# First query group: its value spans cut out of the row tiles by TensorE instead of loaded from memory, in another issue sequence

## The chip, the cores and the metric

The kernel runs on one core of a Trainium2 chip. The metric is the device time of one execution in microseconds (us). Shorter is better.

The engines are TensorE (PE in the profile, its weight loads PEld), VectorE (DVE), ScalarE (ACT), GpSimd (POOL) and SyncE (SP), which here issues all DMAs.

## The reference

Attention with a local window and pooled blocks, followed by a feed-forward layer with softplus, all in float32 (the weights of the second part arrive as 64-bit floats).

```python
batch, n_heads, seq, head_dim = 4, 8, 768, 64
block, window = 32, 16
k_sum = k.reshape(B, H, nb, block, D).max(axis=3)
v_sum = v.reshape(B, H, nb, block, D).mean(axis=3)
scores_l = scale * q @ k^T          # kept where abs(i - j) < 16, else -1e9
scores_s = scale * q @ k_sum^T + log(block)
a = softmax(concat(scores_l, scores_s))
attn = a @ concat(v, v_sum)
x = attn as (3072, 512)
out = softplus(x @ w_in) @ w_out    # w_in 512 x 2048, w_out 2048 x 512
```

## The kernel before

**Tiles.** Queries go in chunks of 256 (three to a batch, twelve in all), heads in pairs (`hp`, four pairs, so 128 rows hold two heads). Two chunks make a group `x` (six groups). Inside a chunk each window of 64 queries sees a span of 96 keys and the 24 block sums of its batch, so that a score row has 120 columns. One attention block treats one chunk and two head pairs. For the first group there are four such blocks, in this order: chunk 0 with head pairs 0 and 1 (called **A0** here), chunk 1 with the same pairs (**A1**), then chunks 0 and 1 with head pairs 2 and 3 (**B0**, **B1**).

**One block.** PE writes scores (`sc`, L642), DVE adds the mask and finds the maxima (L655, eight instructions), ACT takes exponentials (L663, eight), DVE inverts the sums (L670, L671), DVE or POOL normalizes (L676; ACT in eight steps at L679). For the first group PE transposes with an identity (`pt`, L696), ACT copies the result to SBUF (`pT`, L700), PE multiplies with the values (`xo`, L740), ACT rounds the result into `xw` (L770) and DVE writes the rest beside it (L774). Later groups transpose in squares by DVE and a round trip through memory (`tb`, `squares`).

**The first group's inputs.** `FirstPlaces` loads per head pair the queries (L556, 256 KiB) and the eight value spans of two chunks (L564): seven that lie 64 rows apart and one at the start, as a DMA of 336 KiB and one of 48 KiB, eight DMAs in all, 1536 KiB, in runs of 512 bytes. The 24 block means of v come from `declare_first_values`: six row tiles `vn0` of 128 x 512 (L424, 256 KiB each, also in runs of 512 bytes, so all of batch 0's v is in SBUF once), six matmuls with a 0/1 matrix that add up each 32 rows (`vt`, L429), one scaled copy (L440, `v0`), and per head pair a copy of that 24 x 128 block beside each of its eight spans (L570, 24 x 1024 elements). Keys come as `kf0` (L404, 384 KiB per head pair).

**Feed-forward.** For a group, `ph` (L1058) is x @ w_in for one of 16 row blocks `f` of the hidden layer, 12 matmuls with three rounding terms; ACT takes the softplus twice (`gh` rounded at L1160, exact at L1164), DVE the difference (`gl`, L1168), and `po` (L1175) is the product with w_out. Weights are loaded in pairs (L918, L911: 512 KiB or 1024 KiB) and unpacked from 64 bits by DVE, ACT and POOL. Half of the weights is loaded at the start, beside the first group's inputs; the first group's `ph` follows block B1 at once.

**Order.** `SEQUENCE` is a list of numbers: it names each step, and with a letter the engine that takes it. It fixes the order on every engine and on SP's queue. Each engine runs its own list in order and waits at the first step whose input is missing. SP's DMAs use eight semaphores in turn, so that a DMA is issued only when the eighth one before it has landed. `warm` (L1249) are 40 matmuls without use, placed in gaps of PE. The banks `po` (four, also used by `pt` and `xo`) and `ph` (two) are PSUM.

Of the kernel before, what the change touches and what calls it, by code (L numbers as in the profile page):

```python
# [152 lines left out]
98 179 97 185 85 83 113 138 99 106 324 211 114 186 204a 325 326a 372 115 350 42 103 116 227 126b 117 187a 369 127 200a
129 212 327 201 217 128 130 386 351 131 120 118 188a 387b 134 132 352 119 328 121 133 139 135 228 373 214 353 246 202
370 146 371a 140 385 247 248 374 249 250 376 203 255 392a 229 256 257 329 395 251 378 205 258 315 317 321 330 259 354b
355 262 320 396 263 143a 316 215 380 332 232 206 207 375a 218 318 331 414b 269 230 149 264 270 252 253 254 265 377
141a 260 271 356 272 397 266 219a 261 333 381 273 382 398 413 343 357 346 420a 267 360 216 220 415a 221 334 276 399b
336 231 359 379 345 423 348 358 223 222 277 344 400 349 507 508b 283 284 233 512a 424 224 268 236 401 278 279 509b 280
285 286 515 361 237 425 287 234a 235 388 383a 426 533 384 147 534a 274 362 402 389 290 535b 538a 238a 405 391 225 403
291 427a 226a 239 428 390 393 394 404 516 297 298 292 275 293 541 294 406 240 299 241 338a 429 142 687 144 242 243 281  # L160
430 407a 282 300 517 560b 301 364a 244a 431 432 518 519b 245 366 433 411a 566a 561b 416 288 422 289 520 412a 542 417
418 543 295 296 302 419 408 421 559 434 150 337 569 409a 521 410a 435a 367 439 365 304 305 437 339a 510 306a 511 522
524 544 588b 309a 310a 440a 438a 545b 303 525 441 442 587 443 594a 546 450 514 523 570 589 444 451 145 452 513 453 597
571 148 445 307a 526 681 547 685 527a 536 454 689 446 572 540 699 548 682 447 686 457 573a 705 551 683 690 458 698 539
550 549 448 529a 537 464 574 598 449 455 459 700a 460 684 465 466 456 462 575 467 693 599 461 552 468 562 708 688a 576
600 471 601 530a 727 691 553a 567 565 472 563 478 473 602 709 694 479 578 463 557a 564 726 531 728a 532a 474 480 481
475 482 555a 710 469 579 733 577 470 363 692a 711 568 736 755 756b 580 485 712a 581 151 603 754 486 476 713 759 604
605 477 590 585 606 595 586 596 558a 492 593 335 583a 487 493 488 737 591 738 489 494 528 739 483 584 592 495 607 762
608 484 740b 490 491 695 556a 714 308 781a 496 498 785 715 696 609 611a 613a 612a 614a 782b 701 718 436 615 616 617
780 741 703 311 763 618 497 499 716 697 500 501a 624 625 504a 930 502 764 619 702 620 742 707 717 631 765 766 788 610  # L170
626 621 767 873b 622 934 632 627 628 638 789 879 872 704 639 874b 633 634 640 635 882 505a 641 706 901a 928 642 719
623 629 768 902 743 790 791 645 646 729 732 931a 731 647 630 648 720 722 745 636 554 734 730 746 637 649 724a 744 735
932 747 900 929 936 748 652 792 653 757 793 883 643 884 769 758 772 770 644 933 885 907a 659 886 654 503 655 752 660
771 656 661 937 650 662 760 794 761 773 774 910 938 940 795 721 935 651 663 798 666 797 945 778 783 657 658 667 946b
786 784 664 796 787 665 887 750 939 799 911 947a 952 912 888 955 913 875 723 668 776a 889 973 941 669 881 506 914b 876
670 779 751a 753a 800a 804a 725 777 974b 890 880 878 802a 671 975a 805 892 803a 877 806 815 675a 807 891 808 915 809
956 916 816 817 980a 810 672 818 673 983 893 917 674 957 919 1068 819 678a 822 582 894a 903 920 679a 1067 676 906 1069
942 811 918 823 958 959a 812 908 909 904 960 984 829 813 985 824 1072a 986 830 825 814 895 775 826 943 820 987 831 832
896 905 821 827 961 921 833 1399 948 944 988 989 1075 922a 1076 1077 1078 1079 962 951 836 837 680 1080 843 844 838
845 954 964 949 1092b 846 839 1096a 898 953 965 1093 840 963 1091 828 834 835 841 677 950 1099 899 847 801 1100 926a  # L180
1116 966 976 990 967a 993 982 842 848 849 969 971a 1117a 979 1122a 897a 972 968 850 851 1101 981 1115 924a 925 852 853
977 857 858 854 991 992 855 859 978 1081 1102 994 860 995 1533 749 1125 1103a 1070 970 856 997a 1400 927a 999 861 1082
996 1085 862 1071 1074 1084 1104 866 1000 998a 864 1142 1001 865 1002 1003 1141 1010 1073 1004 923 869a 1148a 870 1011
1012 863 1083 1013 1105 1126 1143 1005 1014 1151 1086 1127 867a 1094 1006 1087 1007 1128 1089 1090 1097 1095 1401a
1129 1088 1106 1008 1098 1109 1017 1018 1019 1020 1024 1025 1021 1026 1130 1152 1027 1108 871 1009 1031 1032 1033
1534a 1028 1107 1034 1035 1131 1015 1110 1405 868 1402 1153 1154 1111 1113 1539 1016 1118 1114 1132 1124 1022 1023
1112 1038 1039 1535 1133 1045 1040 1135 1409 1041 1155b 1029 1119 1121 1120 1123 1042 1030 1156 1046 1134 1136 1047
1157 1048 1139 1036 1144 1037 1146 1049 1145 1052 1406 1137 1158 1053 1412 1043 1054 1150 1161 1055 1056 1160 1140
1149 1147 1536 1044 1159 1050 1543 1138 1540a 1051 1058 1059 1162 1057 1163 1165 1164 1061 1064 1166 1167 1168 1176
1169 1177 1060 1170 1178 1171 1225 1062 1172 1183 1184 1179 1226a 1180 1190 1243 1185 1065 1191 1244 1173 1245 1174  # L190
1227 1261 1228 1229 1246 1192 1186 1175 1193 1187 1194 1248a 1181 1247 1266 1234 1197 1182 1204 1205 1198 1262 1239a
1410a 1249 1230 1188 1066 1189 1250 1195 1252 1280 1063 1235a 1263 1264 1236 1265 1253a 1237 1238 1240 1231 1199 1267
1200 1206 1232 1196 1270 1251 1201 1207 1233a 1208 1211 1212 1281a 1282 1268 1218 1213 1214 1257a 1283 1202 1271 1203
# [39 lines left out]
def kernel(  # L233
# [301 lines left out]
    class FirstPlaces:  # L535


        def __init__(self, hp, sums, own, sp):
# [4 lines left out]
            def place(g):  # L543
                return own[g]().rearrange("p two n c -> p (two n c)")
# [803 lines left out]
```

## Time and profile before

| | us |
|---|---|
| three runs | 627.8, 628.35, 630.74 |
| median | 628.35 |
| the profiled execution, whole time | 630.65 |
| its span, first to last instruction | 628.9 |
| PE busy | 607.4 (97% of the span) |
| DVE / ACT / POOL busy | 387.8 / 349.3 / 179.9 |

The page gives busy times over the whole span. The first 60 us hold the loading and attention of the first group, and there no engine is busy all the time; from then on PE is.

### The profile page before, as it was taken

To read this page: it belongs to the slowest core of one execution; us is meant where nothing else is said; L and a number is where in the kernel's file an instruction comes from. 1 tells how busy PE (TensorE), PEld (TensorE's weight loads), DVE (VectorE), ACT (ScalarE), POOL (GpSimd) and SP (SyncE) were. 2 spreads that over 40 slices of the span, in tenths; PEclk is the share of its full clock that TensorE was granted. 3 is DMA by queue.
4 is the path that set the end of the run, shared out by engine and by line. 5 is a ranking of instruction groups with operands and counts; after the bars stand their busy time and mean duration, and the time that the engine had idled before them with its cause. 6 is when DMAs were issued, how large, how long until landed. Compare 5 with 4: busy or idle time off the path is not lost.

```text
span 628.9 us, 12000 instructions
## 1 busy us (share of the span) xinstructions
PE 607.4 (97%) x4452; PEld 507.5 (81%) x4452; DVE 387.8 (62%) x1010; ACT 349.3 (56%) x859; POOL 179.9 (29%) x180
## 2 busy tenths in 40 slices
PE   7669999999999999999999999999999999999997
PEld 6357778787887888888888888889889888989895
DVE  5989988676455765444225579874665664464542
ACT  4799999869567677556436887442212322132211
POOL 5334354041323213121000644474410224103000
PEclk9987999999999999999999999999999999999999
DMA  8997877977857776657435640023040240030031
GB/s 292 289 271 211 226 223 229 267 213 222 265 170 249 204 225 219 206 170 233 132 91 190 194 172 3 1 82 111 10 168 2 100 134 1 27 108 1 31 105 67
DMA packets 66570, 96.12 MB, mean 153 GB/s; under 512 B 5872, under 2 KB 44624, under 8 KB 65744
## 3 DMA queue, kind: packets, MB, share of 16 engines
q1 hardware_dynamic: 66512, 95.36, 49.2%
q8 instruction: 35, 0.57, 0.4%
q14 instruction: 23, 0.19, 0.1%
HBM read 66.06 MB, written 27.26 MB: 148 GB/s over the span
## 4 chain that ended last, share of the span: by engine, by line
PE 82%; ACT 7%; SPq 4%; DVE 4%; DMA 3%; issue 1%; ACTq 0%; DVEq 0%
PE po L1175 39%; PE ph L1058 21%; PE hx L1098 9%; PE hy L1098 7%; PE xo L740 3%; ACT sp L663 2%; PE sc L642 2%; DMA kf<-kT_dram 1%; ACT sp L679 1%; SPq L721 1%; SPq L556 1%; DVE sp L655 1%; DMA st<-v_hp_dram 1%; DMA squares<-tb 1%; SPq L424 1%
## 5 line engine op out<-in xcount | busy, mean ns | idle before, releaser
L1175 PE MATMUL po<-w,gh 128*128 128x512 f32 x768 | 206.4, 397 | 0.0
L1175 PEld LDWEIGHTS po<-w,gh 128*128 128x128 f32 x768 | 141.6, 188 | 31.8 <-issue 0.6
L1058 PE MATMUL ph<-xw,w 128*128 128x512 f32 x672 | 164.4, 396 | 0.0
L1058 PEld LDWEIGHTS ph<-xw,w 128*128 128x128 f32 x672 | 126.9, 190 | 29.1 <-issue 0.3
L1175 PE MATMUL po<-w,gl 128*128 128x512 f32 x384 | 116.1, 396 | 0.0
L1175 PEld LDWEIGHTS po<-w,gl 128*128 128x128 f32 x384 | 71.0, 188 | 15.9 <-issue 0.3
L663 ACT ACTIVATE sp<-sp,nm 128x120 f32<-128x120 f32 x192 | 73.1, 384 | 4.9 <-DVE nm L655 4.6
L1160 ACT ACTIVATE gh<-hx 128x512 fp32r<-128x512 f32 x20 | 12.0, 598 | 108.1 <-DVE hx L1108 108.1
L961 POOL TENSOR_TENSOR t<-t,raw 128x1024 int32<-128x1024 int32 (+1 forms) x20 | 41.9, 2100 | 96.0 <-DVE t L947 74.8
L1168 DVE TENSOR_TENSOR gl<-ph,gh 128x512 fp32r<-128x512 f32 x56 | 38.1, 686 | 46.3 <-ACT ph L1164 46.0
L1160 ACT ACTIVATE gh<-ph 128x512 fp32r<-128x512 f32 x56 | 33.3, 597 | 48.3 <-PE ph L1058 47.9
L802 POOL TENSOR_TENSOR x<-r,x 128x512 fp32r<-128x512 f32 x23 | 30.5, 1336 | 68.3 <-DVE x L795 58.6
L655 DVE CUSTOM_DVE_ANT_0 sp<-sc,added 128x120 f32<-128x120 f32 x192 | 40.9, 277 | 4.1 <-PE sc L642 3.3
L663 ACT ACTIVATION_READ_ACCUMULATOR sp<-sp,nm 128x1 f32 x192 | 36.3, 189 | 0.0
L1098 PE MATMUL hx<-x,w 128*128 128x256 f32 x240 | 35.6, 284 | 0.0
L1098 PE MATMUL hx<-x,sw 128*128 128x256 f32 x240 | 35.4, 283 | 0.0
L1098 PEld LDWEIGHTS hx<-x,w 128*128 128x128 f32 x240 | 32.8, 189 | 2.4
L1160 ACT ACT_TABLE_LOAD x23 | 29.5, 1283 | 8.9 <-PE ph L1058 8.6
L1098 PE MATMUL hy<-x,sw 128*128 128x256 f32 x240 | 34.0, 282 | 0.0
L1164 ACT ACTIVATE ph<-ph 128x512 f32<-128x512 f32 x56 | 33.0, 591 | 0.0
L1098 PEld LDWEIGHTS hx<-x,sw 128*128 128x128 f32 x240 | 31.8, 188 | 0.9
L709 DVE STREAM_TRANSPOSE tb<-sp 128x1024 f32<-128x1024 f32 x20 | 24.8, 1239 | 11.2 <-ACT sp L679 5.8
(113 smaller groups left out, 837.1 us busy)
## 6 DMA issues: line engine op xcount, KB each, us to landing
squares<-tb SPq DMA_DIRECT2D x20, 512.0 KB
pT<-squares SPq DMA_DIRECT2D x80, 128.0 KB
raw<-w_out_dram SPq DMA_DIRECT2D x16, 512.0 KB
kf<-kT_dram SPq DMA_DIRECT2D x16, 384.0 KB
raw<-w_in_dram SPq DMA_DIRECT2D x6, 1024.0 KB
q<-qT_dram SPq DMA_DIRECT2D x20, 256.0 KB
raw<-r SPq DMA_DIRECT2D x20, 256.0 KB
part<-ob SPq DMA_DIRECT2D x10, 512.0 KB
```

The source lines that it names most:

```text
L655: nc.vector.tensor_tensor_reduce(out=sp()[:, n], in0=unit(n), in1=added()[:, kinds.index((lows[w], lows[w + 1]))], scale=-SCALE, scalar=FL ...
L663: nc.scalar.activation(sp()[:, n], sp()[:, n], AF.Exp, bias=nm()[:, n:n + 1], scale=-1.0, accum_out=ss()[:, n:n + 1],)
L709: nc.vector.transpose(out=tb().rearrange("p k (u q) -> p u k q", q=SQ), in_=tiles.sp().rearrange("p u (k q) -> p u k q", q=SQ),)
L740: nc.tensor.matmul(xo()[h * D:(h + 1) * D, g * CH + w * QW:g * CH + (w + 1) * QW], lhsT=tiles.v(g)[:, w, h * D:(h + 1) * D], rhs=queries(g ...
L802: engine.tensor_tensor(to(1), a(), to(0).bitcast(F32), op=ALU.subtract)
L961: nc.gpsimd.tensor_tensor(a, a, word(0, I32), op=ALU.add)
L1058: nc.tensor.matmul(ph(), lhsT=lhs(part, cc), rhs=xw[cc][0]()[:, xw[cc][1], a], start=cc == 0 and n == 0, stop=cc == NCC - 1 and n == 2,)
L1098: nc.tensor.matmul(to()[:, half], lhsT=lhs(wa, cc), rhs=of_x(xa)[:, cc * CH:(cc + 1) * CH], start=cc == 0 and m == 0, stop=cc == NG - 1 an ...
L1160: nc.scalar.activation(gh(), all_of(), AF.Softplus)
L1164: nc.scalar.activation(all_of(), all_of(), AF.Softplus)
L1168: nc.vector.tensor_sub(out=gl(), in0=all_of(), in1=gh().bitcast(F32))
L1175: nc.tensor.matmul(po[t](), lhsT=a()[:, t * P:(t + 1) * P], rhs=w2()[:, part, i2 * DM:(i2 + 1) * DM], start=f == f0 and i == 0, stop=f == ...
```

## The change

The identity (128 columns) becomes the middle third of a tile `shifts` with 384 columns that is zero elsewhere. A matmul whose weights are 96 columns of it, shifted by the distance of a span from a row tile, picks the span's rows out of the tile. Per span one or two row tiles are touched: over the eight spans 1 + 7 x 2 = 15 matmuls, each for all four head pairs (512 columns) at once. Each span then lies in PSUM as 96 x 512 and is copied to SBUF once (eight copies, DVE 5, ACT 3). The eight DMAs of L564 go. The copy of the block means is now made for two spans and all head pairs at a time, again four copies of 24 x 1024, all on ACT (before three on ACT, one on POOL).

```diff
-    ident = Buffer(order, const, [P, P], F32, "ident")
+    shifts = Buffer(order, const, [P, 3 * P], F32, "ident")
...
+            for w, start in enumerate(starts):
+                span = buffer([P, DM], F32, "span", "po", NT, psum)
+                held = range(start // P, (start + KW - 1) // P + 1)
+
+                def window_v(span=span, held=held, start=start):
+                    for i in held:
+                        c0 = P + start - P * i
+                        nc.tensor.matmul(
+                            span()[:KW], lhsT=shifts()[:, c0:c0 + KW], rhs=parts[i](),
+                            start=i == held[0], stop=i == held[-1],
+                        )
+                order.add(PE, 0.95 * len(held), window_v, [shifts, *(parts[i] for i in held)], [span])
+
+                def put(copy, span=span, w=w):
+                    copy(out=place_of(w)[:KW], in_=span()[:KW])
...
-                    def load_v(g=g, w=w, n=n):
-                        nc.sync.dma_start(out=v(g)[:KW, w:w + n], in_=value_windows(0, hp + g, starts[w], n))
-                    order.add(SP, 0, load_v, [], [v_keys[-1]], size=48 * KiB * n, row=512)
...
-0 3 4 5 6 7 8 9 10 11 12 13 14 153 154 2 43 162 15 16 17 18 19 20 21 22 23 24 25 26 27 28 1 29 30 31 32 33 313a 163a
+0 3 4 5 6 1 7 51 53 161 162a 166 197 202 8 9 10 11 64 163 66 164 12 2 13 14 15 16 17 18 19 52 170 165 55 160 171 43
```

The whole sequence is new, to the end of the program. Three places of it follow. Numbers behind a name, as in `kf_211`, tell buffers of one kind apart and mean nothing else.

On SP's queue, the stretch that ends with the last inputs of blocks B0 and B1. Before (13th DMA on; the two `kf` and the `first<-qT` are keys and queries of head pairs 2 and 3, `vn` row tiles, `raw` weights, `first<-v` the spans):

```order
L404 DMA kf_211<-kT_dram 128x768
L404 DMA kf_213<-kT_dram 128x768
L918 DMA raw<-w_in_dram 128x4x256
L424 DMA vn_264<-v_hp_dram 128x4x128
L424 DMA vn_266<-v_hp_dram 128x4x128
L556 DMA first<-qT_dram 128x2x256
L911 DMA raw<-w_out_dram 128x1024
L564 DMA first<-v_hp_dram 96x7x128
L564 DMA first<-v_hp_dram 96x128
L491 DMA q<-qT_dram 128x512
```

And now (11th DMA on):

```order
L946 DMA raw<-w_in_dram 128x4x256
L946 DMA raw<-w_in_dram 128x2048
L430 DMA vn_321<-v_hp_dram 128x4x128
L430 DMA vn_323<-v_hp_dram 128x4x128
L408 DMA kf_327<-kT_dram 128x768
L408 DMA kf_329<-kT_dram 128x768
L939 DMA raw<-w_out_dram 128x1024
L600 DMA first<-qT_dram 128x2x256 x2
L540 DMA q<-qT_dram 128x512
```

The last row tiles now stand ahead of the keys of head pairs 2 and 3, and so does a 1024 KiB load of weights; the spans are gone.

On ACT, the stretch from the exponentials of the second group's first block to the last `pT` of B1. Before:

```order
L663 ACTIVATE sp,ss<-sp,nm 128x120 x8
L700 COPY pT<-pt 120x512
L570 COPY first<-v_351 24x1024
L700 COPY pT<-pt 120x512
L679 ACTIVATE sp_392<-sp_392,ss 128x120 x8
L935 ACTIVATE t<-raw 128x1024
L700 COPY pT<-pt 120x512 x2
```

And now, from the `pT` of A0 on (`sp_439` is block B0, then B1; the one plain `sp` the second group's block):

```order
L728 COPY pT<-pt 120x512 x2
L691 ACTIVATE sp_439,ss<-sp_439,nm 128x120 x8
L798 CAST xw<-xo 128x256 x2
L728 COPY pT<-pt 120x512 x2
L691 ACTIVATE sp_439,ss<-sp_439,nm 128x120 x8
L798 CAST xw<-xo 128x256
L728 COPY pT<-pt 120x512 x2
L798 CAST xw<-xo 128x256
L691 ACTIVATE sp,ss<-sp,nm 128x120 x8
L547 COPY k<-kf_327 128x3x96
L547 COPY k<-kf_327 128x96
L728 COPY pT<-pt 120x512 x2
```

The copies of means, the normalization in eight steps and the unpacking of weights have left this stretch. Four unpacking steps of 128 x 1024 now stand behind the last `xw` and ahead of the first softplus.

On PE, from the product of B0 to the first `po`. Before:

```order
L740 MATMUL xo<-pT,first 64x64 x16
L696 MATMUL pt<-ident,sp_392 120x128 x8
L740 MATMUL xo<-pT,first 64x64 x16
L1058 MATMUL ph<-xw,w 128x512 x24
L642 MATMUL sc<-k,q 64x120 x16
L1175 MATMUL po<-w,gh 128x512 x2
```

And now:

```order
L1280 MATMUL warm<-ident 128x128 x11
L768 MATMUL xo<-pT,first 64x64 x16
L1280 MATMUL warm<-ident 128x128
L724 MATMUL pt<-ident,sp_439 120x128 x8
L1280 MATMUL warm<-ident 128x128 x2
L768 MATMUL xo<-pT,first 64x64 x16
L1280 MATMUL warm<-ident 128x128 x2
L670 MATMUL sc<-k,q 64x120 x16
L1086 MATMUL ph<-xw,w 128x512 x24
L1203 MATMUL po<-w,gh 128x512 x2
```

Of the 40 `warm` matmuls 31 stood at the start, now 9; eleven stand ahead of B0's product, and a block of scores has moved ahead of `ph`.

## Rows read from the trace of the kernel before

**Rows 1.** The page's busy line of PE, then the busy times in three stretches of the span (columns: stretch, length, busy us and count of PE, PEld, DVE, ACT, POOL, then PE's granted clock as a share of full speed, the DMA engines' busy share, GB/s).

```profile
PE 607.4 (97%) x4452; PEld 507.5 (81%) x4452; DVE 387.8 (62%) x1010; ACT 349.3 (56%) x859; POOL 179.9 (29%) x180
...
40.00:53.00 13.00, 8.46 (x109) 7.05 (x107) 12.32 (x24) 12.55 (x38) 6.76 (x6) 0.60 0.77 258
...
60.00:110.00 50.00, 49.82 (x459) 39.53 (x458) 44.65 (x127) 47.81 (x137) 23.04 (x18) 1.00 0.79 226
110.00:624.00 514.00, 512.50 (x3398) 432.58 (x3396) 292.84 (x715) 256.05 (x578) 132.15 (x121) 1.00 0.42 132
```

**Rows 2.** The chain of work that ended last, in order of time (start, length, what): two of its pieces.

```profile
12.97 7.47 DMA kf<-kT_dram
...
51.15 1.97 PE xo L740 x32
```

**Rows 3.** What PE's product with v waited for in the first 70 us (total, times, longest).

```profile
PE xo L740 <- ACT first L570: 1.7, 1, 1.7
PE xo L740 <- ACT pT L700: 1.7, 2, 1.0
```

**Rows 4.** PE's instructions in order of time (start, length, line, operation, out<-in, shape, count; in brackets the idle time before). A float32 matmul of the program shows as two records.

```profile
1.36 8.97 PE L1249 MATMUL warm<-ident 128*128 128x128 f32 x62 [1.36 <-POOL ident masks.py:199]
...
14.88 1.90 PE L429 MATMUL vt<-vn,ones 128*24 128x512 f32 x4
...
25.08 1.04 PE L429 MATMUL vt<-vn,ones 128*24 128x512 f32 x2 [0.29 <-DMA vn<-v_hp_dram]
...
36.07 1.04 PE L696 MATMUL pt<-ident,sp 128*120 128x128 f32 x8
...
38.11 1.17 PE L740 MATMUL xo<-pT,first 120*64 120x64 f32 x32 [1.01 <-ACT pT L700]
```

**Rows 5.** PE again, from the first `ph` on.

```profile
53.05 7.33 PE L1058 MATMUL ph<-xw,w 128*128 128x512 f32 x24
60.31 1.05 PE L642 MATMUL sc<-k,q 64*64 64x120 f32 x32
...
62.08 4.11 PE L1058 MATMUL ph<-xw,w 128*128 128x512 f32 x17
```

**Rows 6.** SP's DMA issues in order of time, two that had waited for a landing: the 25th and the 27th DMA.

```profile
26.24 0.35 SPq L918 DMA_DIRECT2D raw<-w_in_dram  x1
...
29.96 0.35 SPq L911 DMA_DIRECT2D raw<-w_out_dram  x1
```

**Rows 7.** What SP's queue waited for at those two issues (total, times, longest): the 17th DMA (queries of head pair 3) and the 19th (the first 336 KiB of spans).

```profile
SPq L911 <- DMA first<-v_hp_dram: 1.6, 1, 1.6
...
SPq L918 <- DMA first<-qT_dram: 0.9, 1, 0.9
```

**Rows 8.** Two stretches of 5 us, columns as in rows 1.

```profile
5.00:10.00 5.00, 5.00 (x46) 5.00 (x46) 2.82 (x9) 1.25 (x2) 1.60 (x8) 1.00 0.99 366
...
25.00:30.00 5.00, 3.58 (x106) 2.50 (x108) 4.95 (x21) 4.87 (x14) 1.03 (x1) 1.00 1.19 230
```

**Rows 9.** ACT's instructions in order of time, columns as in rows 4. They overlap, so that what one takes of the queue is the distance to the start of the next. The row at 30.68 is the first of a block's eight exponentials, that at 33.72 follows the eighth.

```profile
26.62 0.59 ACT L440 ACTIVATE v<-vt 24x512 f32<-24x512 f32 x1
27.25 1.04 ACT L570 COPY first<-v 24x1024 f32<-24x1024 f32 x1
...
30.68 0.40 ACT L663 ACTIVATE sp<-sp,nm 128x120 f32<-128x120 f32 x1
...
33.72 0.56 ACT L700 COPY pT<-pt 120x512 f32<-120x512 f32 x1
...
37.47 1.06 ACT L700 COPY pT<-pt 120x512 f32<-120x512 f32 x2
38.43 0.38 ACT L770 CAST xw<-xo 128x256 fp32r<-128x256 f32 x1
38.69 1.18 ACT L935 ACTIVATE t<-raw 128x1024 f32<-128x1024 f32 x1
39.74 0.39 ACT L770 CAST xw<-xo 128x256 fp32r<-128x256 f32 x1
...
51.98 0.64 ACT L498 COPY k<-kf 128x96 f32<-128x96 f32 x2
...
56.86 1.28 ACT L1160 ACT_TABLE_LOAD   x1
58.16 0.60 ACT L1160 ACTIVATE gh<-ph 128x512 fp32r<-128x512 f32 x1
```

**Rows 10.** DVE's instruction on the first keys of head pair 2, and a `gl`.

```profile
20.47 0.95 DVE L351 TENSOR_REDUCE ks<-kf 128x24 f32<-128x768 f32 x1 [1.13 <-DMA kf<-kT_dram]
...
59.27 0.69 DVE L1168 TENSOR_TENSOR gl<-ph,gh 128x512 fp32r<-128x512 f32 x1
```

**Rows 11.** Two stretches of 1 us around the fall and the return of PE's clock, columns as in rows 1.

```profile
42.00:43.00 1.00, 0.54 (x16) 0.57 (x20) 1.00 (x4) 1.00 (x7) 0.93 (x1) 0.84 0.98 265
...
56.00:57.00 1.00, 1.00 (x5) 0.78 (x5) 0.99 (x3) 0.98 (x6) 0.00 (x0) 0.83 1.06 332
```

**Rows 12.** What PE waited for after the first 60 us (total, times, longest), all of it.

```profile
PE xo L740 <- DMA st<-v_hp_dram: 1.0, 1, 1.0
PE xo L740 <- DMA v<-vs: 0.3, 1, 0.3
PE xo L740 <- DVE gl L1168: 0.2, 1, 0.2
```

More of the change, by code (lines that the diff above doesn't have):

```diff
@@ L153 @@
[L153 to L157, printed above, removed]
@@ L441, in declare_first_values, with place, place_of, spread @@
             order.add(ACT, act(DM, True), mean, [total], [kept])
+            starts = [s for c in groups[0] for s in win_starts(chunks[c][1])]
+            self.places = [sums_of(n, "first") for n in range(NHP)]
+            per = len(starts) // NHP
+            def place(n):
+                return self.places[n]().rearrange("p two n c -> p (two n c)")
+            def place_of(w):
+                c0 = DM + w % per * DM
+                return place(w // per)[:, c0:c0 + DM]
+            self.place, self.place_of, self.per = place, place_of, per
+            for w, start in enumerate(starts):
[11 more added lines that the diff above has]
+                    copy(out=place_of(w)[:KW], in_=span()[:KW])
+                order.add(
+                    ACT, act(DM, True), lambda f=put: f(nc.scalar.copy), [span], [(self.places[w // per], "v", w)],
+                    ways=[Way(DVE, dve(DM), lambda f=put: f(nc.vector.tensor_copy))],
+                )
+            for n in range(NHP):
+                def spread(copy, n=n):
+                    src = kept()[KW:KS].rearrange("n (o c) -> n o c", o=1)
+                    to = place(n)[KW:KS, DM:DM + per * DM].rearrange("n (w c) -> n w c", c=DM)
+                    copy(out=to, in_=src.broadcast_to([NB, per, DM]))
+                order.add(
+                    POOL, pool(per * DM), lambda f=spread: f(nc.gpsimd.tensor_copy), [kept], [(self.places[n], "sums")],
+                    ways=[
+                        Way(DVE, dve(per * DM), lambda f=spread: f(nc.vector.tensor_copy), port=True),
+                        Way(ACT, act(per * DM), lambda f=spread: f(nc.scalar.copy)),
+                    ],
+                )
         def keep_first(self):
@@ L1254 @@
         order.group = f"a0.0.{hp}"
-        own = [sums_of(hp + g, "first") for g in range(NG)]
-        places = FirstPlaces(hp, sums, own, scratch(f"w{'io'[hp // NG]}{HALF // 2 - 1}", "sp0"))
+        places = FirstPlaces(hp, sums, scratch(f"w{'io'[hp // NG]}{HALF // 2 - 1}", "sp0"))
         for i, tiles in enumerate(places.tiles):
```

203 lines of the change are left out of this document (104 added, 99 removed), and 5 rows, old and new, of the table SEQUENCE.

## The prediction

> **What bounds the kernel now.** I read the busy times by stretch first. Once past 60 us PE is never idle for long: 49.82 of 50 us, then 512.50 of 514 [rows 1], and all its waits there sum to 1.5 us [rows 12]. What PE has to do from the first `ph` on is the same in both kernels, so the time is decided by when that `ph` begins and by how well PE is fed after it. The list of what PE waited for says what holds the first group's products up: ACT's copies of the means and of the transposed probabilities [rows 3]; no wait there names a load of spans. The chain that ended last runs through the keys of head pairs 2 and 3, which are on their way until 20.4 [rows 2], through DVE's sum over them at 20.47 [rows 10], then through DVE and ACT to the product of B1 at 51.15 [rows 2]; `ph` follows at 53.05 [rows 5]. ACT is busy 12.55 of the last 13 us of it [rows 1]. So the bound of the head is ACT's queue, which got its last inputs late. In that stretch PE is granted 0.60 of its clock, that is, mostly the lower of its two levels (1.2 and 2.4 GHz).
>
> **The loads.** Eight DMAs go, 1536 KiB or 1.57 MB: 4.3 us at the 366 GB/s of the stretch 5 to 10, 6.8 us at the 230 GB/s of 25 to 30, in which they ran [rows 8]. But they stood behind the keys and queries of head pair 3, so they delayed no input of a block; what stood behind them is weights, for which PE does not wait. Taken alone their removal is worth nothing at the end, as long as ACT's queue covers it. The new order puts more ahead of the last inputs. In KiB along SP's queue: the sixth row tile ends at 6400 in both kernels, and landed by 25.1 [rows 4]. The queries of head pair 3 ended at 6656 and had landed by 26.24; the first spans, at 7504, by 29.96 [rows 6, 7]; that is 228 KiB per us. Now those queries end at 8192. At 228 they land at 33.0, at the faster stretch's 366 GB/s (357 KiB per us) at 30.5. The second w_out block ends at 7680: 30.7 or 29.1, say 30.
>
> **TensorE.** Two float32 matmuls of 512 columns took 1.90 us [rows 4], so one is 0.95, and fifteen are 14.3 us. Nine lie ahead of A1's scores, where PE waited for loads anyway, and take the place of `warm` matmuls (0.29 each, 31 of them in 8.97 us [rows 4]). Six, 5.7 us, come behind the means' last sum, which needs the sixth row tile: 25.1 + 0.95 + 5.7 + 0.6 for two `warm` gives 32.3, the scores of B0 take some 1.3 (two thirds of a block at 1.05 for the keys, and as much again for the sums' own small matmuls, my estimate), so 33.6, and the eight transposes of A0 1.04 [rows 4]: 34.6. With queries at 33.0, of which the second half of the scores has need, it comes out the same.
>
> **ACT.** A0 is through by about 21 (its scores need the first two queries, at 4096 KiB). ACT then waits for a 1024 KiB weight block at 5888 KiB, which by the two landings at 4992 (20.4) and 6400 (25.1) is there at 23.4, unpacks one step (1.05) and does A1's exponentials (3.04): 27.5. From rows 9: the scaled means 0.6, a copy of means 1.04, and a wait for w_out to 30; two steps of half the size and a small one 1.4, a copy 1.04, one step 1.05, two copies 2.1: 35.6. So ACT's own queue (35.6) is later than PE's transposes (34.6), and that is where the path lies. Then, without a gap: `pT` of A0 0.96, exponentials of B0 3.04, two `xw` 0.5, `pT` 0.96, exponentials 3.04, `xw` 0.25, `pT` 0.96, `xw` 0.25, exponentials of the second group 3.04, a copy of keys 0.6, `pT` of B1 0.96: 14.6, so 50.2. In the kernel before this was 51.5 (start 51.15, on half of the last `pT`).
>
> **From there to the feed-forward.** The product of B1 takes 1.17 at the full clock [rows 4] in place of 1.97, two `warm` 0.6, a block of scores 1.0: `ph` at 53.0. The 24 `ph` took 7.33 while the clock came back only in the stretch 56 to 57 [rows 5, 11]; at the later pace, 4.11 for 17, they take 5.8: 58.8. Before it was 60.31, with as many blocks of scores done. That is 1.5 us. The first `po` needs ACT's softplus: ACT has its last `xw` at 52.0, then four unpacking steps (4.2), the table load 1.28, `gh` 0.5 and the exact one, and DVE's `gl` 0.69 [rows 9, 10], about 59.4, where PE is at 59.3 after the first two `po`: 0.1 lost. I take 1.5 us.
>
> The eight new copies out of PSUM (a 512-wide copy of ACT was 0.59 [rows 9]; DVE has none in the rows, bounded by 0.4 and 0.95, half and all of its 768-wide sum) are 1.8 us on ACT, all before A1, where it waits for loads, and 2 to 5 us on DVE. DVE has them before the mask of B1; it must reach the mask of B0 by 35.6 minus 1, and by the same counting is there at about 33.6, so its cover is 1 us. The larger memset on POOL is ahead of anything that needs it by microseconds: it can cost at most some 0.5 us at the start, where loads are awaited.
>
> **Clock.** PE's clock fell in the stretch 42 to 43, in which PE was busy for 0.54 us, and rose in 56 to 57 after steady work [rows 11]. In the new order eleven `warm` (3.2 us) stand just ahead of B0's product, so the gaps from 40 to 50 shrink to 1 to 1.5 us. I take the full clock, and keep the other as a rival. The Trainium skill, "TensorE: Matmul & The Clock Gate", section "What's actually happening", says "the default state is throttled, and activity releases the throttle"; the rows of 42 to 57 agree. By that rule the shorter opening run of `warm` speaks against this change; the row at 1.36 cannot tell, since there the clock was full from the first.
>
> **The rivals.**
> (1) *The bytes come off the path.* If the head is bound by the DMA engines as a whole, the 4.3 to 6.8 us come off: 5.5 in the middle, 622.8. For it: the engines' busy share is 0.99 and 1.19 in the two stretches [rows 8]. Against it: the waits named by PE are on ACT, and the first inputs stand later in the queue. The Trainium skill, "DMA: Bandwidth & Descriptors", section "Specifications", gives line rate from 512 B per transfer on, so by it the spans ran at full rate; by its 358 GB/s for one core they were worth 4.4 us, an estimate from that page. The 230 GB/s of 25 to 30 speak against it.
> (2) *Slower: B0 and B1 start too late.* The path is then loads, PE, `pT` of A0. If the whole queue to 8192 KiB moved at 228 KiB per us from 2 us on, the queries land at 38, `pT` of A0 starts at 39 in place of 35.6, and 3.4 less 1.5 is 1.9 slower. If from the keys of head pair 2 to the last `pT` it took as long as before (20.4 to 51.5, 31 us), with those keys at 6784 KiB, hence 26.8: 57.9, 7.7 late, 6.2 slower. The middle is 4: 632.4. It begins to cost when those queries land after 34.4, turns the sign after 36, and shows from 39 on.
> (3) *The clock falls all the same.* B1's product 1.97, `warm` and scores doubled (3.2), `ph` 7.33: 62.7 in place of 60.31, 2.4 slower: 630.7.
> (4) *The new order starves PE later.* ACT and DVE are at 47.81 and 44.65 of 50 us from 60 to 110 [rows 1], and waits were only 1.5 us. Three times that costs 3 us and eats the gain: 629.9.
>
> **How the numbers follow.** The sum is made on the profiled execution, 630.65, which is 2.3 us above the median of three, 628.35. 630.65 - 1.5 = 629.15; against the median, 626.8. Chances: this forecast 0.47 (its own range 624.3 to 628.8, from the two ends of the w_out landing and one unpacking step either way), (1) 0.12, (2) 0.16, (3) 0.13, (4) 0.12. 0.5% is 3.1 us, about what a measurement of this kernel can tell from no change. Faster by that is (1) and about a quarter of the forecast's own range: 0.25. Slower is two thirds of (2) and small parts of (3) and (4): 0.17. The rest, 0.58, is no difference. The range goes from (1) to the middle of (2): 622.8 to 632.4.
>
> **What would show it.** Right: `pT` of A0 on ACT at 35 to 36.5 with ACT busy from there to the last `pT` near 50; PE's clock at 1.00 from 20 us on; 24 `ph` in 5.8 us, ended near 59; waits of PE after 60 us near 1.5 us. Wrong: a wait of PE or ACT on the queries or keys of head pair 3 (rival 2), a clock of 0.5 between 42 and 56 (rival 3), waits of PE on `gl`, weights or `v` after 60 us that sum to over 3 us (rival 4), `ph` begun before 50 (rival 1).

## The result, and the profile after

The changed kernel took 635.03 us in the median of five runs (634.13 to 636.08); the kernel before, beside it, 630.74 (627.8 to 631.52). The ratio is 1.0089, with a 95% interval of 1.0071 to 1.0108: slower by 0.7 to 1.1%, where 626.8 was forecast and 632.4 was the upper end of the range. The profiled execution took 636.08, its span 634.0 against 628.9, so that 5.1 of its 5.4 us lie inside the span.

PE's busy time went up by 11.9 us, to this (the page's busy line):

```profile
PE 619.3 (98%) x4482; PEld 508.5 (80%) x4482; DVE 401.8 (63%) x1024; ACT 337.5 (53%) x832; POOL 175.7 (28%) x177
```

**The opening came out better than forecast.** PE's spans, then PE from B1's product on (columns as in [rows 4, 5], to which these rows answer):

```profile
24.66 1.88 PE L467 MATMUL span<-vn,ident 128*96 128x512 f32 x4
...
47.93 1.15 PE L768 MATMUL xo<-pT,first 120*64 120x64 f32 x32
...
50.63 5.85 PE L1086 MATMUL ph<-xw,w 128*128 128x512 f32 x24
56.32 0.66 PE L1203 MATMUL po<-w,gh 128*128 128x512 f32 x2
60.11 0.79 PE L1203 MATMUL po<-w,gl 128*128 128x512 f32 x1 [3.13 <-DVE gl L1196]
60.70 5.59 PE L1086 MATMUL ph<-xw,w 128*128 128x512 f32 x18
...
68.22 4.34 PE L1086 MATMUL ph<-xw,w 128*128 128x512 f32 x18
```

The first and the last copies of transposed probabilities on ACT [rows 9]:

```profile
32.54 1.07 ACT L728 COPY pT<-pt 120x512 f32<-120x512 f32 x2
...
47.21 1.07 ACT L728 COPY pT<-pt 120x512 f32<-120x512 f32 x2
```

The 24 `ph` begin at 50.63 and end at 56.5, where the kernel before ended them at 60.4 [rows 5]: 3.9 us ahead. Then PE has two matmuls and stands for 3.1 us, and the next 18 `ph` take 5.59 us, where the 18 from 68.22 on take 4.34. The busy times by stretch (columns as in [rows 1, 11]) show why: after 57 to 60 with PE idle, the granted clock is at the lower of its two levels (0.50 to 0.52 from 60 to 63).

```profile
20.00:40.00 20.00, 19.15 (x314) 12.00 (x310) 18.78 (x74) 19.79 (x63) 10.70 (x7) 1.00 0.73 226
40.00:53.00 13.00, 11.86 (x170) 10.65 (x167) 12.48 (x48) 12.43 (x42) 9.27 (x8) 1.00 0.65 227
53.00:57.00 4.00, 3.98 (x17) 2.77 (x16) 0.61 (x5) 3.90 (x7) 1.31 (x1) 1.00 0.95 232
57.00:60.00 3.00, 0.00 (x0) 0.00 (x0) 3.00 (x6) 2.98 (x7) 0.00 (x0) 1.00 1.05 238
60.00:61.00 1.00, 0.89 (x2) 0.80 (x3) 1.00 (x2) 0.99 (x6) 0.00 (x0) 0.52 1.02 310
...
63.00:64.00 1.00, 1.00 (x5) 0.82 (x4) 0.97 (x2) 0.98 (x3) 0.90 (x1) 0.77 0.67 258
64.00:65.00 1.00, 1.00 (x6) 0.78 (x6) 1.00 (x1) 0.61 (x1) 0.92 (x2) 1.00 0.14 50
```

The first loads came faster than in the kernel before. Its stretch 25 to 30 had 230 GB/s, with the span loads in it [rows 8]; the same stretch now, with no span load:

```profile
25.00:30.00 5.00, 5.00 (x14) 1.88 (x12) 4.97 (x10) 4.88 (x9) 2.06 (x1) 1.00 1.08 358
```

What DVE did before the `gl` that PE waited for, in order of time:

```profile
56.70 0.95 DVE L355 TENSOR_REDUCE ks<-kf 128x24 f32<-128x768 f32 x1 [3.38 <-DMA kf<-kT_dram]
57.57 0.68 DVE L967 TENSOR_SCALAR t<-t 128x1024 f32<-128x1024 f32 x1
58.17 0.69 DVE L993 CAST w<-t 128x1024 fp32r<-128x1024 f32 x1
58.77 0.69 DVE L967 TENSOR_SCALAR t<-t 128x1024 f32<-128x1024 f32 x1
59.37 0.68 DVE L1196 TENSOR_TENSOR gl<-ph,gh 128x512 fp32r<-128x512 f32 x1
```

DVE stood 3.4 us before a maximum over the first keys of the second batch, which were not there; the `gl` came four steps behind it in DVE's list. SP's queue shows where those keys had been (issues in order of time, then the wait of its queue):

```profile
39.82 8.21 SPq L939 DMA_DIRECT2D raw<-w_out_dram  x2
...
48.55 0.90 SPq L371 DMA_DIRECT2D kf<-kT_dram  x2
```

```profile
SPq L939 <- PE pt L724: 7.3, 1, 7.3
```

A w_out load waited for B1's transposes, the keys queued behind it, and the first of their two loads landed 8.1 us after its issue. In the kernel before, these keys were issued at 38.87 and 40.60. That could not stay: they use the memory of the first group's places, and a place now holds two spans of *all* head pairs, so that the place of these keys is free after the product of B0 (46.2), where a place of one head pair was free after A1.

**What PE waited for after 53 us** (total, times, longest), the whole list; it answers to [rows 12], whose sum was 1.5:

```profile
PE po L1203 <- DVE gl L1196: 3.1, 1, 3.1
PE xo L768 <- DMA pT<-squares: 0.8, 1, 0.8
PE hx L1126 <- DVE p L1146: 0.7, 1, 0.7
PE xo L768 <- DMA v<-vs: 0.4, 1, 0.4
PE xo L768 <- issue: 0.4, 1, 0.4
PE ph L1086 <- DVE gl L1196: 0.3, 1, 0.3
PE xo L768 <- DMA v<-v_hp_dram: 0.2, 1, 0.2
```

**A ledger by place.** Each later group's attention product `xo` is the same work in both kernels. PE's start there, less the start in the kernel before, less the work that one order puts ahead of it and the other does not (0.233 us for a matmul of `ph` or `po`: in the kernel before, 24 `ph` took from 62.08 to 67.66), says how late PE is. Thus the last of these 20 products began at 323.54 against 320.52, with three `po` more ahead of it: 3.02 - 0.70 = 2.3 us late. The same at the first of them gives 76.45 - 72.88 - 12 x 0.233 = 0.8, and PE's last matmul ended at 629.5 against 625.1, 4.4 late. The span adds 0.7 behind it. So the profiled execution lost 0.8 up to 73 us (3.9 gained, more than that given back at the `gl` and at the low clock), 1.5 between 73 and 323, 2.1 between 323 and PE's end, 0.7 behind PE's end. Most of the loss lies behind the opening, in steps that the edit itself does not touch. The 0.3 us outside the span stays unexplained.

### The profile page after: what moved, and what is told of

It reads as the page before. It is cut to its first block, busy times and chain, and to the rows that moved or that the text cites. A ratio compares the mean times of both kernels' runs of the same rounds, so it can differ in the third digit from the quotient of the medians.

```text
span 634.0 us, 12050 instructions
## 1 busy us (share of the span) xinstructions
PE 619.3 (98%) x4482; PEld 508.5 (80%) x4482; DVE 401.8 (63%) x1024; ACT 337.5 (53%) x832; POOL 175.7 (28%) x177
## 4 chain that ended last, share of the span: by engine, by line
PE 82%; DMA 6%; DVE 5%; SPq 3%; ACT 2%; issue 1%; POOL 0%; DVEq 0%; ACTq 0%; POOLq 0%
PE po L1203 37%; PE ph L1086 20%; PE hx L1126 9%; PE hy L1126 7%; PE xo L768 3%; PE sc L670 3%; DMA raw<-w_out_dram 1%; DMA kf<-kT_dram 1%; PE span L467 1%; SPq L749 1%; DMA v<-vs 1%; DVE sp L683 1%; SPq L562 1%; DMA v<-v_hp_dram 1%; DMA q<-qT_dram 1%
## 5 line engine op out<-in xcount | busy, mean ns | idle before, releaser
L1196 DVE TENSOR_TENSOR gl<-ph,gh 128x512 fp32r<-128x512 f32 x56 | 38.1, 683 | 56.6 <-ACT ph L1192 56.5
L830 POOL TENSOR_TENSOR x<-r,x 128x512 fp32r<-128x512 f32 x23 | 32.1, 1401 | 127.5 <-ACT x L823 65.0
L989 POOL TENSOR_TENSOR t<-t,raw 128x1024 int32<-128x1024 int32 (+1 forms) x20 | 41.9, 2099 | 77.5 <-DVE t L975 54.2
L704 POOL TENSOR_TENSOR sp<-sp,ss 128x960 f32<-128x960 f32 x10 | 18.2, 1822 | 65.9 <-DVE ss L699 60.7
L1126 PE MATMUL hx<-x,w 128*128 128x256 f32 x240 | 35.6, 284 | 0.1
L1126 PEld LDWEIGHTS hy<-x,sw 128*128 128x128 f32 x240 | 31.3, 189 | 0.9 <-DVE u L1136 0.3
```

The costliest lines, as they stand in the source:

```text
L830: engine.tensor_tensor(to(1), a(), to(0).bitcast(F32), op=ALU.subtract)
L989: nc.gpsimd.tensor_tensor(a, a, word(0, I32), op=ALU.add)
L1126: nc.tensor.matmul(to()[:, half], lhsT=lhs(wa, cc), rhs=of_x(xa)[:, cc * CH:(cc + 1) * CH], start=cc == 0 and m == 0, stop=cc == NG - 1 an ...
L1196: nc.vector.tensor_sub(out=gl(), in0=all_of(), in1=gh().bitcast(F32))
```

## The experiments

Three theories. *Wait theory*: the loss starts at the keys before the first `gl`. *Product theory*: the 15 matmuls are the loss. *Order theory*: the rest of the new sequence feeds PE worse. Further theories are explained in the expectations that name them. In a sequence a number is a step and a letter its engine.

The ledger of all runs that were profiled, in us against the kernel before (its profiled execution: 630.65, span 628.9):

| run | PE late at 73 | at 106 | at 320 | at its end | span | profiled time | median | ratio to before, 95% |
|---|---|---|---|---|---|---|---|---|
| changed | +0.8 | +2.1 | +2.3 | +4.4 | +5.1 | 636.08 | 635.03 | 1.0071 to 1.0108 |
| changed, e9 | -2.1 | -0.5 | -1.4 | +0.9 | +1.6 | 632.58 | 634.24 | 1.0058 to 1.0092 |
| e1 | -1.4 | -0.2 | +0.5 | +2.7 | +3.4 | 634.41 | 634.53 | 1.0051 to 1.0086 |
| e2 | -1.3 | +1.0 | +1.6 | +3.9 | +4.6 | 635.30 | 634.91 | 1.0060 to 1.0103 |
| e3 | -2.0 | -0.6 | +0.6 | +2.5 | +3.2 | 634.26 | 635.13 | 1.0059 to 1.0093 |
| e4 | -2.2 | -1.5 | -1.1 | -0.2 | -0.2 | 630.46 | 632.13 | 1.0016 to 1.0050 |
| e5 | -1.4 | -0.1 | +1.7 | +2.4 | +2.4 | 633.05 | 631.99 | 1.0016 to 1.0053 |
| e6 | -0.9 | +4.1 | +3.9 | +4.1 | +4.1 | 634.77 | 633.94 | 1.0042 to 1.0090 |
| e7 | -2.0 | -0.2 | +0.4 | +2.2 | +2.1 | 633.17 | 633.13 | 1.0036 to 1.0069 |
| e8 | +11.9 | +12.2 | +11.8 | +11.8 | +11.8 | 642.43 | 644.04 | 1.0193 to 1.0249 |
| e10 | -0.7 | -0.4 | -0.6 | +1.6 | +2.3 | 633.08 | 632.63 | 1.0035 to 1.0070 |
| e11 | -1.0 | +4.4 | +4.5 | +4.7 | +4.7 | 635.38 | 634.41 | 1.0059 to 1.0097 |
| e12 | -0.6 | +3.6 | +3.8 | +4.7 | +4.7 | 635.34 | 635.34 | 1.0077 to 1.0108 |
| e13 | -1.5 | -1.1 | -2.0 | -1.7 | -1.7 | 628.93 | 630.55 | 0.9987 to 1.0016 |
| e14 | -1.1 | +0.3 | -0.4 | +1.8 | +2.5 | 633.56 | 635.80 | 1.0054 to 1.0101 |

One profile is one execution; the executions of a kernel spread over 0.9 us (e1) to 6.3 us (the kernel before beside e5), so the ledger tells where time went and the medians what it came to. Its zero, 630.65, is a slower execution of the kernel before than most (its medians beside the experiments are 629.45 to 630.35), so an entry can be some 1 us too low.

**e1, the maximum behind the `gl`** (377 is the maximum over the first keys, 258 the first `gl`):

```diff
-359 255 377 228 222 144 223a 209 378 256 263 257 258 264
+359 255 228 222 144 223a 209 378 256 263 257 258 377 264
```

> DVE's maximum over the first keys of the second batch moves behind the first `gl`; nothing else changes. Wait theory (the loss starts where DVE stands before keys that are not there, and takes PE's clock with it): PE's wait for that `gl` falls from 3.1 us to under 1 us, the granted clock from 60 to 64 stays at 1.00, and 3.5 to 4.5 us come back: 630.5 to 631.5 where the changed kernel had 635.0. Product theory (the 15 matmuls that TensorE does in addition are the loss): the wait may go, but the time stays within 1 us of 635.0. Order theory (most is lost after 70 us, by the rest of the new issue sequence): the wait goes and at most 2 us come back, 633 to 635.

DVE's rows and PE's wait in its profile:

```profile
56.89 0.69 DVE L1195 TENSOR_TENSOR gl<-ph,gh 128x512 fp32r<-128x512 f32 x1 [0.50 <-ACT ph L1191]
57.50 0.94 DVE L354 TENSOR_REDUCE ks<-kf 128x24 f32<-128x768 f32 x1
```

```profile
PE po L1202 <- DVE gl L1195: 0.5, 1, 0.5
```

The wait went from 3.1 to 0.5 and ends on ACT; PE is 1.4 ahead at 73 us. This profile is no test of the wait theory, though: by the landing events in its trace the keys were there at 54.3, and e9 below has the same 0.5 with nothing edited. The six executions are the test. In none of them can the first `gl` wait for the keys; they spread over 0.9 us only, and their median fell by 0.5, not 4. So late keys are not the loss: the order theory had this right.

**e2, the spans loaded in the new sequence:**

```diff
-                order.add(PE, 0.95 * len(held), window_v, [shifts, *(parts[i] for i in held)], [span])
...
-                def put(copy, span=span, w=w):
-                    copy(out=place_of(w)[:KW], in_=span()[:KW])
+                def put(w=w, start=start):
+                    src = v_hp[self.b, :, start:start + KW].rearrange("hp s c -> s hp c")
+                    nc.sync.dma_start(out=place_of(w)[:KW].rearrange("s (hp c) -> s hp c", c=P), in_=src)
+                order.add(SP, 0, put, [], [(self.places[w // per], "v", w)], size=192 * KiB, row=512)
```

> The new issue sequence, but the eight spans are loaded again (eight DMAs of 192 KiB behind the queries of head pair 3) and the 15 matmuls and eight copies are gone. Wait theory: the 3.1 us before the first `gl` and the low clock behind them remain, since keys and weights are loaded as before them; the time is within 1.5 us of 635.0, more if the loads hold up A0's product. Product theory: the time falls to that of the kernel before, 5 us less, about 630. Order theory: as the wait theory, no gain.

634.91: no change. With 1536 KiB of loads back and 14 us of PE's work gone, the new sequence costs the same, so the product theory, which had 630, falls. (Here the wait for the first `gl` was 0.5: the keys happened to land in time.) The span loads slow the queue where they run, from 26 us on, behind the queries of head pair 3:

```profile
25.00:30.00 5.00, 4.67 (x75) 2.47 (x73) 3.66 (x7) 3.70 (x10) 2.06 (x1) 1.00 1.20 218
```

**e3, the keys ahead of the w_out load** (244 the load, 376 and 380 the keys):

```diff
-185 186a 244 335 139 41 350 326 42 140 142 376 143 212 380 129
+185 186a 335 139 41 350 326 42 140 142 376 143 212 380 244 129
```

> On SP's queue the load of w_out's fourth pair, which waits for B1's transposes, moves behind the first two key loads of the second batch; nothing else changes. Wait theory: the keys are issued when the last reader of their place (the product of B0, ended at 46.2) is done instead of at 48.55, so they land near 54.5 instead of 56.7, the wait for `gl` falls from 3.1 to about 1 us, and 2 to 3.5 us come back: 631.5 to 633. Product theory: no gain, within 1 us of 635.0. Order theory: at most 1.5 us. If the keys still land after 56 the load engines, not SP's queue, set their time.

SP's row of the keys, and DVE's maximum over them, which now follows the mask without a wait:

```profile
46.41 0.80 SPq L370 DMA_DIRECT2D kf<-kT_dram  x2
```

```profile
53.58 0.95 DVE L354 TENSOR_REDUCE ks<-kf 128x24 f32<-128x768 f32 x1
```

They are issued at 46.41, as expected, and PE is 2.0 ahead at 73 us; at 320 it is 0.6 behind, and the median (635.13) has not moved. What the opening gains is lost later.

**e4, the old tail** (from here on the steps in the order and on the engines of the kernel before):

```diff
-1173 1174 1172 1175 1067 1418a 1070a 1176 1177 1233 1178
+1173 1174 1172 1175 1414 1420 1544 1551 1548a 1067 1072
```

> The new sequence up to the product of the last attention block (at 323 us), and behind it every remaining step in the order, and on the engine, of the kernel before. Wait theory: what is lost before 70 us stays, and the time is within 1 us of 635.0. Order theory: PE ends its work 2.5 us sooner against the last attention product, and the last piece behind PE is 0.6 us shorter: 632 to 632.5. Product theory: no gain.

632.13, which is 2.1 to 3.0 less than the versions with the new tail (635.03 and 634.24 unedited, 634.53 and 635.13 in e1 and e3), and the tail's own loss falls from 2.1 + 0.7 to 0.8 + 0.0 in the ledger. The order theory's number. How the 0.7 arises is seen in the last rows of PE and DVE, first of the changed kernel, then the same reads here:

```profile
629.06 0.40 PE L1203 MATMUL po<-w,gl 128*128 128x512 f32 x1
```

```profile
627.39 1.39 DVE L1233 TENSOR_TENSOR ob<-po,ob 128x512 f32<-128x512 f32 x2 [0.68 <-PE po L1203]
629.49 1.29 DVE L1233 TENSOR_TENSOR ob<-po,ob 128x512 f32<-128x512 f32 x2 [0.71 <-PE po L1203]
```

```profile
622.80 2.79 DVE L1232 TENSOR_TENSOR ob<-po,ob 128x512 f32<-128x512 f32 x4 [6.85 <-PE po L1202]
```

In the new order PE ends its four banks in the order 3, 0, 2, 1 and DVE reads them in the order 3, 0, 1, 2: the third read waits for the last product, and two reads stand behind PE's end instead of one.

**e5, e1's edit and e4's together.**

> Two edits together: DVE's maximum over the second batch's first keys behind the first `gl`, and the order of the kernel before for all that follows the last attention product (323 us). Order theory (the loss is the later part of the new sequence, and in some executions the late keys as well): the old tail gives 2.9 us as alone, and the moved maximum keeps every execution in the lower half of what the old tail alone gave (630.5 to 635.4): 630.5 to 631.5 where the kernel before has 630.35. If the two do not add: 632 and more. Product theory (TensorE's added matmuls): 634 to 635.

631.99: they do not add up, and the executions (629.88 to 634.8) are not confined to the lower half. In its profile 3.1 us went between 73 and 320, half of it in one wait for `v<-vs` at 122 us.

**e6, e11 and e12, the old order from 84, 87 and 98 us on** (e1's edit kept). The joints:

```diff
 e6   392 369 -408 516b 520a 294 432 +151a 157 149a 344 408 516b
 e11  242 243 -370 433 695 283 289 +157 149a 344 409 523
 e12  253 437 -424 309 426 152a 568a +157 155 150 152 438
```

> As the run before it, but the order of the kernel before already from the second attention product of the second group on (84 us), so that only the opening is new. Order theory: what the new sequence loses between 85 and 323 us (some 2 us with the moved maximum, against the same point in the kernel before) does not arise, the lead of 1.4 us that the opening has at 84 us lasts to the end: 628.5 to 629.5, just under the kernel before. Layout theory (the edit itself loses, since places that all head pairs share come free later): the loss from 85 to 323 us comes back in the old order too, 630.5 to 632.

> The new opening with the moved maximum, then the order of the kernel before from about 87 us, joined some steps later than where the two orders lay further apart and a wait of 3.0 us arose at the joint. Order theory: without that wait the lead of 1.4 us is there at 96 us, later waits are those of the old order (1 to 1.5 us in both), and the end is as the kernel before or up to 1.5 us faster: 628.5 to 630. If the joint stalls again, PE's list shows a wait of over 1 us between 85 and 100.

> The same with the joint at about 98 us. Order theory: as the run before it less what the new sequence loses up to 98 us (0.4 to 0.6 us in the earlier runs): 629 to 630.5, about the kernel before. If the joint is the place of loss again, a single wait of over 1 us shows there.

All three stalled at the joint, e6 and e12 as follows (PE's waits), e11 with 2.2 and 1.0 us:

```profile
PE sc L669 <- DVE nm L682: 3.0, 1, 3.0
```

```profile
109.31 1.77 PE L767 MATMUL xo<-pT,v 120*64 120x64 f32 x32 [3.59 <-ACT sp L690]
```

No lead reached the old order, so none of the three says whether it would have kept one: their use for that is nil. What they do show is that the old order loses at most 0.2 us between 106 and 320 when PE comes late.

**e7, the last two products exchanged** (2066 and 2067, two of PE's last four):

```diff
-2068 2065 2067 2066 2076 2070 2078 2071 2072 2075
+2068 2065 2066 2067 2076 2070 2078 2071 2072 2075
```

> The changed kernel with two of PE's last four output products exchanged, so that they end in the order in which DVE reads their banks. Order theory: DVE's third read no longer waits for the fourth product, one read of 0.69 us less stands behind the last product: 634.3 where the changed kernel had 635.0, the piece from PE's end to the span's end 3.8 in place of 4.5. Others: no difference.

The piece behind PE's end is 0.7 us shorter (+2.2 at PE's end, +2.1 in the span), as expected. The median, 633.13, lies 1.1 below e9's and 1.9 below the first one's; e9's spread lets only the 0.7 be put down to the edit.

**e8, the edit alone in the old order:**

```diff
+52 64 65 202 54 66 67a 68 69 59 61 ... 56 70 71a 58 72 73
```

(64 to 79 are products and copies of spans; 52 to 62 the sums of row tiles. The keys of the second batch go behind B1's product, 139, and their maxima and copies behind the first `gl`, 258.)

> The edit alone: TensorE makes the spans, but every step that the kernel before has stays in its old order and on its old engine, but for the second batch's keys, which cannot be loaded before the last product of the first group has left their place; the maxima and copies of these keys move with them. The spans' matmuls follow the sums of the row tiles, the copies go to ACT and DVE in turn. Order theory: nothing is lost behind 323 us; the opening loses what stands ahead of A0's transposes (some six matmuls, 5.7 us, of which ACT's queue covers part) and gains nothing: 630 to 634. Layout theory: a loss of 2 us or more between 70 and 323 us. Product theory: 635 or more, with no loss of another kind.

644.04, 9 us above the 635 at which the product theory's open range begins, and far above the 630 to 634 of the order theory. All 11.9 us are lost up to the first product of the second group, none between there and 320, none in the tail; so the layout theory, a loss of 2 us or more there, falls. In the opening ACT and DVE wait, in their lists, for spans that PE makes from row tiles that land late (waits up to 70 us: total, times, longest):

```profile
ACT first L473 <- PE span L466: 11.9, 4, 3.5
DVE first L473 <- PE span L466: 10.1, 4, 3.9
```

So the products are not free in themselves: in the old opening, placed as here, they hold up ACT and DVE, and in the new one, rebuilt around them, they do not. That is what the new sequence bought.

**e9, the changed kernel again.**

> The changed kernel once more, nothing edited, on the chip of the runs beside it. If the late keys of the second batch come in some executions only, this profile either shows the wait of 3.1 us for the first `gl` again, with 1.5 to 1.8 us of low clock behind it (634 to 636), or a wait of 0.5 us and a time near 632 to 633. If the wait is there in every execution: 635 again, as recorded.

DVE's rows at the place of the 3.1 us wait:

```profile
54.17 0.95 DVE L355 TENSOR_REDUCE ks<-kf 128x24 f32<-128x768 f32 x1 [0.60 <-DMA kf<-kT_dram]
...
56.99 0.69 DVE L1196 TENSOR_TENSOR gl<-ph,gh 128x512 fp32r<-128x512 f32 x1
```

Issued 0.24 us later than in the first profile, the keys landed 2.5 us sooner. PE waited 0.5 for the `gl`, its clock stayed at 1.00, and it was 2.1 ahead at 73 us. Of the four profiles with this opening unedited one has the long wait (the first; not e4, e7, e9). This execution was the fastest of the six, and was still 1.6 us longer in its span than the kernel before: 0.7 lost from 73 to 320, 2.2 in the tail, 0.7 in the last reads. By the medians, 634.24 against 629.45 beside it, the loss is 4.8.

**e10, the new tail on the kernel before**, no part of the edit:

```diff
-1059 1162 1057 1163 1165 1164 1061 1064 1166 1167 1168
+1059 1162 1057 1163 1061a 1060 1165 1166 1164 1167 1410a
```

> The kernel before (spans loaded, its own order and engines) up to the last attention product, and behind it the changed kernel's order and engines: no part of the edit, only the new tail. Order theory: PE loses some 2 us against its work behind 323 us and DVE's last reads 0.7 us more, 2.5 to 3 us together: 632 to 633.5 where the kernel before has 630. Any theory in which the edit (TensorE's spans, the shared places) makes the loss: no difference, 630.

632.63 against 629.45, as the order theory had it: 2.2 on PE behind 320 us, 0.7 in the last reads. PE's waits there:

```profile
PE hx L1098 <- DVE p L1118: 0.7, 1, 0.7
PE ph L1058 <- DVE gl L1168: 0.3, 1, 0.3
PE hx L1098 <- DVE u L1108: 0.2, 1, 0.2
```

They sum to 1.2 of the 2.2. The list counts a wait from the modelled end of the matmul before, which lies behind the point where the next one usually starts. From start to start it is more, as at the longest of these waits, where six `hy` of 0.12 us each would bring the next start to 491.89:

```profile
491.17 0.88 PE L1098 MATMUL hy<-x,sw 128*128 128x256 f32 x6
492.70 0.96 PE L1098 MATMUL hx<-x,sw 128*128 128x256 f32 x6 [0.66 <-DVE p L1118]
```

That is 0.8 us. Counted so, the three waits are 0.8, 0.4 and 0.4, and a step from `hy` to `hx` at 406.8, too short for the list, is 0.3: 1.9 of the 2.2. What PE loses in the new tail is waits, the named ones all for results of DVE.

**e13, a lead in the old order.** ACT's normalization of B1 left out of the kernel before:

```diff
-            for n in range(NG * NU):
+            for n in range(0 if by_pe else NG * NU):
                 nc.scalar.activation(sp()[:, n], sp()[:, n], AF.Copy, scale=ss()[:, n:n + 1])
```

> The kernel before, with no part of the change; left out are ACT's eight steps that normalize block B1 (2.33 us of ACT's queue ahead of the last `pT`), so that its opening has a lead of about 2 us for PE, as the changed kernel's has when the keys come in time. Order theory (the old middle keeps a lead, the new one loses it): PE is some 2 us ahead of the kernel before at 73 us and still 1.5 us or more at 320 us; time 627.5 where the kernel before has 629.5. Pace theory (from 65 to 120 us ACT, DVE and the loads set the pace, so no order keeps PE's lead): under 1 us of it is left at 120 us, in waits for loads and `gl`; time 629 to 629.5.

The two readings disagree. In the profile PE is 1.5 ahead at 73 us, 1.1 at 117 and 2.0 at 320 (there the 1.0 us wait of [rows 12] for `st` did not occur), as the order theory says. In the medians there is nothing: 630.55 against 629.85, and the profiled execution was the fastest of twelve. Neither forecast is met; this stays open.

**e14, the keys late every time** (378, a load of v, ahead of 376):

```diff
-142 376 143 212 380 129
+142 378 376 143 212 380 129
```

> The changed kernel with the first load of v for the second batch's means moved ahead of its first two key loads on SP's queue, so that these are issued some 2.4 us later and with 384 KiB ahead of them. Late-key theory (the executions of 635 us and more are those in which the keys land after 56 us): every execution now has the wait for the first `gl`, 3 to 6 us, with low clock behind it: 635.5 to 638, none under 635. If the spread has another cause: 633 to 635.5 as the unedited kernel.

The maximum in the profiled execution, the fastest of six, and PE's wait:

```profile
55.37 0.95 DVE L354 TENSOR_REDUCE ks<-kf 128x24 f32<-128x768 f32 x1 [1.79 <-DMA kf<-kT_dram]
```

```profile
PE po L1202 <- DVE gl L1195: 1.5, 1, 1.5
```

The issue came 1.0 us later, not 2.4. The median rose to 635.8, but two of six executions lie under 634 where none was expected under 635. Late keys raise the time; that they are the whole spread of the changed kernel is not shown, and e1, without this wait, has nearly the changed kernel's median.

## Why the prediction was wrong

*The loads.* Their removal was called worth nothing by itself. In the new sequence e2 agrees: the loads back and the products gone came to nothing together. But more than weights stood behind them: in the kernel before PE waited for queries of the second group, issued at 34.79, just as its clock fell [rows 11]:

```profile
42.46 1.72 PE L642 MATMUL sc<-k,q 64*64 64x120 f32 x32 [2.16 <-DMA q<-qT_dram]
```

What that wait cost is not shown. (By the queue's own list the DMAs of [rows 6, 7] are the 26th, 28th, 18th and 20th, one more each than written there; the pairs are right.)

*TensorE and its copies.* 14.3 us were forecast, 13.8 measured, and the cover was there: e2 is no faster without them. In the old opening it was not (e8).

*ACT, and the landings.* The chain was right and its times too late. `pT` of A0 came at 32.54 in place of 35.6: A1's exponentials were done at 25.2, not 27.5, and ACT had no wait for w_out ahead of the copies. The term that was mis-sized is the queue's pace: 228 KiB per us was read where span loads were in flight, and now there were none. By the landing events of the trace the second w_out block was there at 26.4, not 30, and the queries of head pair 3 at 27.9, not 30.5 to 33.0. This is in part rival 1's mechanism, which the forecast had set aside; here it moved the opening and not the end. From the first `pT` to the end of the last it took 15.6 us, where 14.6 were forecast without a gap; 0.55 of the difference is a wait of ACT for B0's transposes.

*`ph` and the clock.* 50.63 in place of 53.0; 24 `ph` in 5.85 us as forecast, on a clock of 1.00 in every stretch from 20 to 57. Up to 56.5 the gain was 3.9 us where 1.5 was taken.

*The first `gl`.* "0.1 lost" counted ACT and the `gl` itself, and left out what stands ahead of that `gl` in DVE's list and who feeds that. The real price was 0.5 where the keys were in time and 3.1 in the first profile. Rival 3 asked for the clock in B1's gaps; it fell instead behind this wait, where 18 `ph` took 5.59 in place of 4.34. The Trainium skill, "TensorE: Matmul & The Clock Gate", section "What's actually happening", says that activity releases the throttle; the stretch 57 to 60 (PE at 0.00 busy) and the 0.52 and less behind it agree.

*The lifetime of the places.* The parts of the change were costed as additions to the opening. That a place now serves all head pairs, and so holds up the second batch's keys, was not seen. The forecast asked of the removed loads what stood behind them on SP's queue; the same question, asked of the w_out load that waits for B1's transposes, would have found the keys.

*The step that failed* is the first paragraph's: what PE does from `ph` on is the same, "so the time is decided by when that `ph` begins and by how well PE is fed after it". The second half was then carried as unchanged, although the whole list is new to the end of the program. Rival 4 named this and was given 0.12 and a price of 3 us. Its mechanism is the one that happened, and it has two places. From 73 to 320 us every profile that keeps the new sequence there loses 0.7 to 3.1 us (changed, e1 to e5, e7, e9, e14; 0.7 to 2.3 already by 106), with waits of PE of 0.2 to 1.5 us for `pT<-squares`, `v` and `gl`; the old order lost -0.5 to 0.1 over the same stretch in e8, e10 and e13. This place rests on the profiles alone: the three runs that should have tested it (e6, e11, e12) stalled at the joint. From 320 us on the new order costs 1.8 to 2.3 us on PE and 0.7 behind it, shown in both directions: taking it out of the changed kernel gave 2.1 to 3.0 us (e4), putting it into the kernel before cost 3.2 (e10). The sum in e9, with no late key: -2.1 + 0.7 + 2.2 + 0.7, that is, 1.5 slower, in that kernel's fastest execution against a slow one of the kernel before. By the medians the whole loss is 4.3 to 4.8 us, of which the tail is some 3.

Open: whether any order would have kept the opening's lead (e13 against its medians), what makes the middle of the new order lose, and what else than the keys spreads the executions. No complete version beat the kernel before; the nearest, e4 and e5, are 0.2 to 0.5% slower.

## What to carry to other kernels

When an edit comes with a new issue order, forecast the order as an edit of its own, to the last instruction: compare what each engine reads last with what finishes last, and look at each wait that had been short. In front of every result that the busiest engine waits for, list what stands ahead of it in its engine's queue, and trace the inputs of those steps too. When a buffer's layout changes, ask which later load uses its memory and when its last reader is now done.

## What the runs showed of the hardware

The same load of 384 KiB (the first of the two of keys), issued at 48.55, 48.79 and 48.69 us in three executions of one opening (the first, e9, e4), was there at 56.7, at 54.2 and before 53.4: 8.1, 5.4 and under 4.7 us after its issue, beside the same neighbours in the queue. PE waited 3.1 us behind the longest flight and 0.5 behind the other two.

With the span loads in flight the DMA engines moved 218 to 241 GB/s at a busy share of 1.18 to 1.20 (25 to 30 us of the kernel before, e2 and e10); without them 358 at 1.08 in the same stretch of the changed kernel. Runs of 512 bytes alone do not explain it: the last row tiles, in the same runs, landed in a stretch (20 to 25 us of the changed kernel) of 371 GB/s. What else of the span loads does is not shown.
